# Moving weight preparation earlier and halving the plain part of the Strassen block

## The chip, the cores and the metric

The kernel runs on one core of a Trainium2 chip. The metric is the device time of one execution in microseconds (us), the median of several runs. All engines named here belong to this core: TensorE (PE, with PEld for its weight loads), VectorE (DVE), ScalarE (ACT), GpSimd (POOL) and SyncE (SP). POOL and SP issue nearly all DMA transfers.

## The reference

Three layers follow each other: a retention layer, and two feed-forward layers over its 3072 tokens of 512 features.

```
for t in range(S):                       # retention, 4 x 8 heads, S = 768, D = 64
    state = gamma * state + outer(k[t], v[t])
    y[t] = scale * (q[t] @ state)
x = y as 3072 tokens x 512
h = x @ w_in;  g = h * sigmoid(1.702 h);  x = g @ w_out      # 512 -> 2048 -> 512
h = x @ w_in2; g = max(h, 0) ** 2;        out = g @ w_out2   # 512 -> 2048 -> 512
```

## The kernel before

**Number format.** Every large matrix product is three matmuls in fp32r: each operand is split into a high part, which ACT casts, and a low part, which DVE subtracts; the kernel adds low x high, high x high and high x low in PSUM. All these matmuls are 128x128 by 128x512.

**Stages.** Tokens are worked in blocks. Blocks 0 and 1 of the first feed-forward layer (512 tokens each) go through `up` and `down`, 16 steps f each, with the products written plainly. From token 1024 on the blocks are 1024 tokens wide and use a Strassen-Winograd scheme with seven products in place of eight: `up2` (eight slice pairs p, seven products of six matmuls each for a pair) and `down2` (28 steps u, 12 matmuls each). These blocks are called (0,1), (0,2) for the first layer and (1,0), (1,1), (1,2) for the second.

**The mixed block (0,1)**, tokens 1024 to 2047, is special. The first `PL` of its eight slice pairs are computed plainly in `up_plain` (four steps of 12 matmuls for a pair), while `mixed_x` makes the Strassen operands of x (B12, B22, T1 to T4: sums on DVE, high parts on ACT at L703, low parts on DVE at L704). The remaining pairs go through `up2`. The high and low parts reuse memory of the up weights, so T2 and T4 can only be placed once plain steps have read those weights.

**The making.** The Strassen sums of the weights are made during the kernel by one generator, `make`, which `background(us)` pushes on: each call first puts the ACT instructions that have been queued with `later` into ACT's program, then adds its argument to a credit and runs the generator's steps until the credit is used up; every step's `yield` names what it takes from the credit. `make_first` prepares the first layer in 16 rounds (steps 0.7, 0.7, 0.85, 0.85, and 1.25 for the low part at L286 and its DMA at L287). `make_second` prepares the second layer from 32 raw chunks. A chunk takes 0.45, 0.7 and 0.7 (L138, L143, L151), then 0.6 and 0.6 (L380 to L384), and 1.1 for the low part (L348) and DMA (L349) of the chunk before. When chunk n is begun, `scale(n + 1)` queues the two ACT instructions (L133, L134) on the next raw chunk; the next call of `background` places them. POOL loads the raw chunks (L275, 512 KB each) and writes the results (L287 1024 KB, L349 896 KB). Chunks 0 and 1 are loaded when `make_first` begins, chunk 2 when `make_second` begins, into memory that `make_first`'s pool has used.

In block 1 `background(BG / 2)` is called twice in each step f below 15. In `up_plain` it is called once after each step, in `up2` twice a slice pair (`BGM` in the mixed block, `BGUP` elsewhere), and in `down2` of the first layer at each step u from 12 on (`BGD`).

**Order.** Every engine executes its instructions in the order in which the program places them; a waiting instruction holds up all that stand behind it. After the last call in block 1 the program places the last step of block 1 (`up` with f = 15: GELU at L655, cast at L656, low part at L660), then the casts and low parts of B11 and B21 (L703, L704), then the first plain step, `down` with f = 15 and `finish`.

**PSUM.** `up`, `up_plain` and `down` use two pools (four banks "h", four banks "y"). After `up_plain` they are closed and one pool "ps" of eight banks opens; `bank` hands its banks out in the order of the queue `banks`.

**Down steps.** In `down2`, `sums(u)` (DVE) runs for u < 12 and the x operands of the next block (`x_operands` through `tick`) from u = 12 on; `prepare` casts the operand of step u + 2 (L980 on ACT, L981 on DVE). From u = 20 the product adds into banks that ACT has just copied out (L1012).

Of the kernel before, what the change touches and what calls it, by code (L numbers as in the profile page):

```python
# [10 lines left out]
F32 = mybir.dt.float32  # L11
# [5 lines left out]
ALU = mybir.AluOpType  # L17
PSUM = bass.MemoryType.PSUM

P = 128  # L20
# [7 lines left out]
TB = 512  # L28
# [12 lines left out]
NSTD = 2  # L41
SLOTS = 8
EARLY = 2
BG = 4.7
BGK = 2.55
BGT = 1.45
CV0 = 7
RAWU = 2
FILL = 6
RAWS = 5  # L50
PL = 4
BGUP = (2.15, 2.4)
BGM = 2.8
BGD = 0.62

# [2 lines left out]
B11, B21, B22, T1, T2, T3, T4, B12 = range(8)  # L60
# [4 lines left out]
def tile_retention_then_two_ffns(  # L65
# [346 lines left out]
    def background(us):  # L412

        credit[0] += us
        while acts:
            acts.popleft()()
        while credit[0] > 0:
            c = next(maker, None)
            if c is None:
                credit[0] = min(credit[0], 3.0)  # L420
                return
            credit[0] -= c
# [21 lines left out]
    with tc.manual_schedule():  # L444
# [254 lines left out]
        def pair(i, src):  # L699
            if i not in xh:  # L700
                xh[i] = wa_p.tile([P, 2, TB], F32R, tag="w0", name=f"xh{i}")
                xl[i] = wb_p.tile([P, 2, TB], F32R, tag="w0", name=f"xl{i}")
            nc.scalar.copy(out=xh[i], in_=src)  # L703
            return lambda: v.tensor_tensor(out=xl[i], in0=src, in1=xh[i], op=ALU.subtract)  # L704
# [83 lines left out]

        g = {}
        ps_p = []  # L790
        banks = deque(range(8))

        def gt(q, p):
            key = q, p // 2
# [4 lines left out]
        def mixed_x():  # L799

            (b11, b21), (b12, b22) = xs.pop(NSTD), xs.pop(NSTD + 1)
            yield
            yield
            yield
            low = pair(B12, b12)
            yield
            low()
            low = pair(B22, b22)
            yield
            low()  # L810
            for _ in range(5):
                yield
            v.tensor_tensor(out=b11, in0=b12, in1=b11, op=ALU.subtract)
            low = pair(T1, b11)
            yield
            low()
            yield
            v.tensor_tensor(out=b11, in0=b22, in1=b11, op=ALU.subtract)
            low = pair(T2, b11)
            yield  # L820
            low()
            yield
            v.tensor_tensor(out=b12, in0=b22, in1=b12, op=ALU.subtract)
            low = pair(T3, b12)
            yield
            low()
            v.tensor_tensor(out=b21, in0=b21, in1=b11, op=ALU.subtract)
            yield
            pair(T4, b21)()

        def up_plain():

            x = mixed_x()
            for c in range(2):
                pairs = ((B11, B21), (B12, B22))[c]
                for s in range(2 * PL):
                    f = NQ * (s % 2) + s // 2
                    hi, lo = weights(f, 0)
                    hp = hp_p.tile([P, TB], F32, tag="h", name=f"h{NSTD + c}_{f}")
                    for k in range(KD):  # L840
                        h, e = (t[pairs[k // 2]][:, k % 2] for t in (xh, xl))
                        nc.tensor.matmul(hp, lo[:, k], h, start=(k == 0), stop=False)
                        nc.tensor.matmul(hp, hi[:, k], h, start=False, stop=False)
                        nc.tensor.matmul(hp, hi[:, k], e, start=False, stop=(k == KD - 1))
                    if c == 0 and s == 0:
                        down(NSTD - 1, NF - 1)
                        finish(NSTD - 1)
                        g_ctx.close()
                        wr_p.extend(
                            ctx.enter_context(  # L850
                                tc.tile_pool(name=f"wr{i}", bufs=1, side="left", reuse_waits="tile")
                            )
                            for i in range(EARLY, SLOTS)
                        )
                    if c == 1 and s == 0:
                        fetch()
                    r, p = divmod(f, NQ)
                    nc.scalar.activation(out=gt(QS[2 * r + c], p), in_=hp, func=ACTF.Gelu_apprx_sigmoid)  # L858
                    if c == 1 and s % 4 == 1 and s > 4:
                        thirds(s // 4 - 1)  # L860
                    next(x, None)
                    background(BGK if c == 0 and s not in (4, 5) or c == 1 and s < 2 else BGT)
            for _ in x:
                pass
            first_ctx.close()
            ps_p.append(ctx.enter_context(tc.tile_pool(name="ps", bufs=1, space=PSUM, reuse_waits="tile")))

        def thirds(m):

            t = g[12, m]  # L870
            v.tensor_tensor(out=t, in0=g[22, m], in1=t, op=ALU.subtract)
# [125 lines left out]
        def down2(l, n, loads, tick):  # L997
            xb, yb, zb = {}, {}, {}
            y = {}
            last = (l, n) == blocks[-1]  # L1000

            def store(q, e):
                r, c = q // 10 - 1, q % 10 - 1
                j = 2 * n + c
                row = 2 * r + e
                dst = ykept[j][:, row] if l == 0 else out[row * P:(row + 1) * P, j * TB:(j + 1) * TB]
                (nc.gpsimd if not last else (nc.sync, nc.scalar)[e]).dma_start(out=dst, in_=y[q][:, e])

            def copy(q, e, a):
                if e == 0:  # L1010
                    y[q] = xy_p.tile([P, 2, TB], F32, tag="xy", name=f"o{l}_{n}_{q}")
                nc.scalar.copy(out=y[q][:, e], in_=a[e][0])  # L1012

            def add(q, e, a):
                v.tensor_tensor(out=y[q][:, e], in0=a[e][0], in1=y[q][:, e], op=ALU.add)
                store(q, e)

            def after(i, e, a):
                if i == 1:
                    yb[e] = bank(f"D{l}_{n}_2_{e}")  # L1020
                    nc.scalar.copy(out=yb[e][0], in_=a[e][0])
                elif i == 2:
                    copy(11, e, a)
                    store(11, e)
                elif i == 6:
                    copy(12, e, a)
                elif i == 7:
                    copy(22, e, a)
                    add(22, e, zb)
                elif i == 4:  # L1030
                    copy(21, e, a)
                    store(21, e)
                elif i == 3:
                    add(12, e, a)

            def free(a):
                for e in range(2):
                    banks.append(a[e][1])

            for i in ORDER:  # L1040
                acc = xb if i in (1, 6, 7, 4) else yb if i == 2 else zb
                if i in (1, 5):
                    for e in range(2):
                        acc[e] = bank(f"D{l}_{n}_{i}_{e}")
                for m in range(NQ // 2):
                    gi, gm, hi, lo = ready.popleft()
                    assert (gi, gm) == (i, m)
                    u = 4 * ORDER.index(i) + m
                    if u % 2 == 1 and u < 8:
                        loads(u // 2)  # L1050
                    if u < 12:
                        sums(u)
                    else:
                        tick()
                    prepare(l, n)
                    if l == 0 and u >= 12:
                        background(BGD)
                    for e in range(2):
                        a = acc[e][0]
                        for p in (2 * m, 2 * m + 1):  # L1060
                            w = fetched[l, n, 1, i, p].rearrange("p j (h c) -> p j h c", h=2)
                            wh, wl = w[:, e, 0], w[:, e, 1]
                            s0, s1 = p == 0 and i in (1, 5), p == NQ - 1
                            matmul(a, wl, hi[:, p % 2], s0, False)
                            matmul(a, wh, hi[:, p % 2], False, False)
                            matmul(a, wh, lo[:, p % 2], False, s1)
                        if m == NQ // 2 - 1:
                            after(i, e, acc)
                    for p in (2 * m, 2 * m + 1):
                        del fetched[l, n, 1, i, p]  # L1070
                    fetch()
                    yield
                if i == 2:
                    free(yb)
                elif i == 3:
                    free(zb)
                elif i == 4:
                    free(xb)
# [112 lines left out]
```

## Time and profile before

| what | value |
|---|---|
| median of 3 runs | 1038.77 us (1038.4 to 1039.32) |
| the profiled execution's own time | 1040.23 us |
| its span, first to last instruction | 1037.9 us |
| mean granted TensorE clock | 0.998 |
| busy: PE, PEld, DVE, ACT, POOL | 99%, 81%, 74%, 55%, 11% |
| 16 DMA engines | 281 MB, 271 GB/s over the span |

The span is what the trace shows; the own time of the same execution is 2.3 us longer, and the median of the runs is 1.46 us below that own time. Busy shares are means over the whole span. PE is nearly always busy, so the idle stretches of PE are few and can be looked at one by one.

### The profile page before, as it was taken

The page shows a single profiled execution, that of the slowest core. Times are in us where ns is not written, and L with a number is a line of the kernel's source. Part 1 is how long each engine was busy: PE and PEld are TensorE (multiplying, and loading weights), DVE is VectorE, ACT ScalarE, POOL GpSimd, SP SyncE. Part 2 cuts the span into 40 slices and gives each one's busy share as a digit, 9 for nine tenths or more (in the row PEclk, how much of TensorE's full clock was granted, in tenths as well). Part 3 has the DMA queues.
Part 4 walks back from the last instruction along what each step waited for, and adds up shares of the span by engine and source line. Part 5 has one row for each costly group of instructions (what it writes and reads, how often), then busy time and mean ns, then how long its engine had stood idle before and what let it go on. Part 6 is the DMA issues. An engine that isn't in the chain of part 4 may idle for free.

```text
span 1037.9 us, 15626 instructions
## 1 busy us (share of the span) xinstructions
PE 1024.2 (99%) x5575; PEld 844.7 (81%) x5575; DVE 769.7 (74%) x1065; ACT 575.1 (55%) x928; POOL 111.4 (11%) x167
## 2 busy tenths in 40 slices
PE   8999999999999999999999999999999999999998
PEld 6888888888878887888887888888888888888886
DVE  5888998798898879567879566787445986355953
ACT  4677775444757566466576588564233464233543
POOL 2121210111321001111001211000000001000000
PEclk9999999999999999999999999999999999999999
DMA  9995798866889888999878999877776877767664
GB/s 349 407 397 175 270 314 298 306 239 239 298 263 354 298 264 268 345 363 343 279 264 272 342 374 294 268 229 232 218 192 194 252 236 232 216 196 195 207 200 162
DMA packets 118812, 281.37 MB, mean 271 GB/s; under 512 B 12624, under 2 KB 12752, under 8 KB 118480
## 3 DMA queue, kind: packets, MB, share of 16 engines
q1 hardware_dynamic: 93488, 187.05, 55.2%
q0 software_dynamic: 24672, 92.28, 25.1%
q8 instruction: 44, 0.72, 0.3%
q10 hardware_dynamic: 576, 1.05, 0.3%
q14 instruction: 32, 0.26, 0.1%
HBM read 206.93 MB, written 73.40 MB: 270 GB/s over the span
## 4 chain that ended last, share of the span: by engine, by line
PE 77%; DVE 4%; ACT 1%; issue 1%; DMA 1%; ACTq 0%; DVEq 0%
PE D L878 34%; PE X L878 19%; PE Z L878 9%; PE Y L878 5%; PE y L681 2%; PE y L679 2%; PE y L680 2%; PE h L648 2%; PE h L650 1%; PE h L649 1%; DVE xl L704 1%; DMA kw<-wq 1%; DVE wq L348 1%; DVE gx L981 1%; DVE w L143 0%
## 5 line engine op out<-in xcount | busy, mean ns | idle before, releaser
L878 PE MATMUL D<-gx,r 128*128 128x512 f32 x1680 | 384.7, 390 | 2.6 <-ACT o L1012 2.4
L878 PEld LDWEIGHTS D<-gx,r 128*128 128x128 f32 x1680 | 314.4, 188 | 71.2 <-ACT o L1012 3.2
L981 DVE TENSOR_TENSOR gx<-g,gx 128x1024 fp32r<-128x1024 f32 x140 | 170.5, 1221 | 41.5 <-ACT gx L980 40.8
L980 ACT CAST gx<-g 128x1024 fp32r<-128x1024 f32 x140 | 145.8, 1051 | 90.3 <-PE D L878 85.5
L878 PE MATMUL X<-xh,r 128*128 128x512 f32 x576 | 177.7, 390 | 0.0
L896 ACT COPY g<-X 128x512 f32<-128x512 f32 x108 | 63.3, 586 | 161.6 <-PE X L878 161.5
L901 DVE TENSOR_TENSOR g<-Z,g 128x512 f32<-128x512 f32 x72 | 49.8, 691 | 134.0 <-ACT g L896 100.7
L878 PEld LDWEIGHTS X<-xh,r 128*128 128x128 f32 x576 | 108.4, 188 | 22.6
L878 PE MATMUL X<-xl,r 128*128 128x512 f32 x288 | 112.1, 389 | 0.0
L878 PE MATMUL Z<-xh,r 128*128 128x512 f32 x288 | 88.6, 389 | 0.0
L878 PEld LDWEIGHTS X<-xl,r 128*128 128x128 f32 x288 | 54.2, 188 | 11.3
L878 PEld LDWEIGHTS Z<-xh,r 128*128 128x128 f32 x288 | 54.1, 188 | 11.2
L878 PE MATMUL Z<-xl,r 128*128 128x512 f32 x144 | 56.0, 389 | 0.0
L648 PE MATMUL h<-hl,w 128*128 128x512 f32 x128 | 50.2, 392 | 0.3 <-DVE w L171 0.2
L649 PE MATMUL h<-hl,w 128*128 128x512 f32 x128 | 49.8, 389 | 0.0
L650 PE MATMUL h<-hl,w 128*128 128x512 f32 x128 | 49.8, 389 | 0.0
L681 PE MATMUL y<-gl,w 128*128 128x512 f32 x128 | 49.8, 389 | 0.0
L679 PE MATMUL y<-gh,w 128*128 128x512 f32 x128 | 49.8, 389 | 0.0
L680 PE MATMUL y<-gh,w 128*128 128x512 f32 x128 | 49.8, 389 | 0.0
L878 PE MATMUL Y<-xh,r 128*128 128x512 f32 x144 | 45.3, 396 | 2.2 <-ACT g L858 2.2
L133 ACT ACTIVATE raw<-raw 128x512 f32<-128x512 f32 x64 | 43.2, 675 | 2.4 <-DMA raw<-win 2.4
L349 POOL DMA_DIRECT2D kw<-wq x32 | 30.4, 950 | 129.0 <-DVE w L381 61.4
(112 smaller groups left out, 1545.5 us busy)
## 6 DMA issues: line engine op xcount, KB each, us to landing
r<-kw SPq DMA_DIRECT2D x532, 256.0 KB, 3.4
kw<-wq POOLq DMA_DIRECT2D x32, 896.0 KB, 6.5
unit<-qkv SPq DMA_DIRECT2D x47, 512.0 KB, 9.1
raw<-w POOLq DMA_DIRECT2D x32, 512.0 KB, 6.2
kw<-wh POOLq DMA_DIRECT2D x16, 1024.0 KB, 4.7
kw<-w SPq DMA_DIRECT2D x16, 512.0 KB, 5.1
raw<-win POOLq DMA_DIRECT2D x16, 512.0 KB, 6.6
raw<-wout POOLq DMA_DIRECT2D x16, 512.0 KB, 6.1
```

The costliest lines, as they stand in the source:

```text
L133: nc.scalar.mul(hm, raw[:, :, 1].bitcast(F32), 2.0 ** -112)
L648: nc.tensor.matmul(hp, lo[:, k], xh, start=(k == 0), stop=False)
L649: nc.tensor.matmul(hp, hi[:, k], xh, start=False, stop=False)
L650: nc.tensor.matmul(hp, hi[:, k], xl, start=False, stop=(k == KD - 1))
L679: nc.tensor.matmul(a, lo[:, e], gh, start=s0, stop=False)
L680: nc.tensor.matmul(a, hi[:, e], gh, start=False, stop=False)
L681: nc.tensor.matmul(a, hi[:, e], gl, start=False, stop=s1)
L878: nc.tensor.matmul(a, w, b, start=start, stop=stop, skip_group_check=True)
L896: nc.scalar.copy(out=t, in_=a)
L901: v.tensor_tensor(out=t, in0=a, in1=t, op=ALU.add)
L980: nc.scalar.copy(out=hi, in_=src)
L981: v.tensor_tensor(out=lo, in0=src, in1=hi, op=ALU.subtract)
```

## The change

`PL` goes from 4 to 2: two slice pairs of the mixed block instead of four are computed plainly, six instead of four go through `up2`. `mixed_x` is written anew for eight steps in place of sixteen: the empty steps go, and T3 comes before T2. The argument of `background` in `up_plain` becomes a list of eight values, one for each step. `BG` for block 1 rises from 4.7 to 5.0. In `down2` of the first layer the calls at u = 12 to 22 get nothing, those below 12 get 0.25 and those from 23 on get 2.2. The pool "ps" gets all its eight banks placed when it opens, in order, and the queue begins with banks 4 to 7. The `thirds` calls inside `up_plain` go; `up2` has its own.

```
-BG = 4.7
-BGK = 2.55
-BGT = 1.45
+BG = 5.0
+BGT = (2.4, 1.3, 0.2, 0.2, 0.2, 2.4, 0.2, 2.0)
-PL = 4
-BGUP = (2.15, 2.4)
-BGM = 2.8
-BGD = 0.62
+PL = 2
+BGUP = (2.2, 2.5)
+BGM = 2.75
+BGD = 2.2
+BGE = 0.25
...
-        banks = deque(range(8))
+        banks = deque((4, 5, 6, 7, 0, 1, 2, 3))
...
             (b11, b21), (b12, b22) = xs.pop(NSTD), xs.pop(NSTD + 1)
-            yield
-            yield
-            yield
             low = pair(B12, b12)
             yield
             low()
             low = pair(B22, b22)
             yield
             low()
-            for _ in range(5):
-                yield
             v.tensor_tensor(out=b11, in0=b12, in1=b11, op=ALU.subtract)
             low = pair(T1, b11)
             yield
             low()
-            yield
-            v.tensor_tensor(out=b11, in0=b22, in1=b11, op=ALU.subtract)
-            low = pair(T2, b11)
-            yield
-            low()
-            yield
             v.tensor_tensor(out=b12, in0=b22, in1=b12, op=ALU.subtract)
             low = pair(T3, b12)
+            yield
+            low()
+            v.tensor_tensor(out=b11, in0=b22, in1=b11, op=ALU.subtract)
+            yield
+            low = pair(T2, b11)
             yield
             low()
...
-                    if c == 1 and s % 4 == 1 and s > 4:
-                        thirds(s // 4 - 1)
                     next(x, None)
-                    background(BGK if c == 0 and s not in (4, 5) or c == 1 and s < 2 else BGT)
+                    background(BGT[2 * PL * c + s])
...
             ps_p.append(ctx.enter_context(tc.tile_pool(name="ps", bufs=1, space=PSUM, reuse_waits="tile")))
+            for k in range(8):
+                ps_p[0].tile([P, TB], F32, tag=f"b{k}", name=f"bank{k}")
...
-                    if l == 0 and u >= 12:
-                        background(BGD)
+                    if l == 0:
+                        background(BGD if u >= 23 else BGE if u < 12 else 0)
```

## Rows read from the trace of the kernel before

**Rows 1.** The page, part 1: busy us, share of the span, instructions.
```profile
PE 1024.2 (99%) x5575; PEld 844.7 (81%) x5575; DVE 769.7 (74%) x1065; ACT 575.1 (55%) x928; POOL 111.4 (11%) x167
```

**Rows 2.** Waits of PE: line, releaser, us in total, times, longest.
```profile
PE Y L878 <- ACT g L858: 2.2, 1, 2.2
```

**Rows 3.** Timeline of PE after the plain steps: start, length, work, idle before.
```profile
302.69 0.39 PE L878 MATMUL X<-xl,r 128*128 128x512 f32 x1
305.27 1.11 PE L878 MATMUL Y<-xh,r 128*128 128x512 f32 x2 [2.20 <-ACT g L858]
...
309.02 0.63 PE L878 MATMUL X<-xh,r 128*128 128x512 f32 x2
```

**Rows 4.** Windows: length, busy by engine, granted clock, DMA share, GB/s.
```profile
305.20:307.00 1.80, 1.73 (x4) 1.38 (x5) 1.80 (x5) 1.55 (x3) 0.21 (x1) 0.56 0.84 264
```

**Rows 5.** Chain that ended last: start, us, work; down steps of three blocks.
```profile
346.61 38.26 PE D L878 x168
...
422.53 1.36 PE X L878 x6
...
501.41 40.95 PE D L878 x180
...
576.61 1.36 PE X L878 x6
...
655.49 73.91 PE D L878 x324
```

**Rows 6.** Chain that ended last, 336 to 432 us: what stands before D.
```profile
390.40 0.77 DVE w L151
...
396.58 1.24 DVE xb L724
...
399.84 0.49 ACT o L1012
```

**Rows 7.** Timeline of DVE at the end of block 1 and after it.
```profile
249.10 1.23 DVE L286 TENSOR_TENSOR wh<-wt,wh 128x1024 fp32r<-128x1024 f32 x1 [0.51 <-ACT wh L324]
...
254.22 2.36 DVE L704 TENSOR_TENSOR xl<-x,xh 128x1024 fp32r<-128x1024 f32 x2 [0.26 <-ACT xh L703]
...
262.62 0.43 DVE L138 TENSOR_SCALAR w<-raw 128x512 uint32<-128x512 uint32 x1 [1.65 <-ACT raw L133]
...
268.06 0.76 DVE L151 SCALAR_TENSOR_TENSOR w<-w,raw 128x512 uint16<-128x512 uint16 x1
```

**Rows 8.** Timeline of POOL over the same stretch.
```profile
250.74 0.75 POOL L287 DMA_DIRECT2D kw<-wh  x1 [2.39 <-DVE w L138]
256.26 0.55 POOL L275 DMA_DIRECT2D raw<-win  x1 [4.77 <-issue]
```

**Rows 9.** Line L287, window 250 to 252 us: its one transfer.
```profile
DMA to landing us min/median/max: 4.9/4.9/4.9
```

**Rows 10.** Line L275, window 255 to 262 us: its one transfer.
```profile
DMA to landing us min/median/max: 5.0/5.0/5.0
```

**Rows 11.** Line L275 over the whole span.
```profile
DMA to landing us min/median/max: 3.9/6.5/9.7
```

**Rows 12.** Timeline of ACT at the end of block 1 and after it.
```profile
253.15 2.00 ACT L703 CAST xh<-x 128x1024 fp32r<-128x1024 f32 x2
...
261.92 0.66 ACT L133 ACTIVATE raw<-raw 128x512 f32<-128x512 f32 x1
...
269.97 0.68 ACT L133 ACTIVATE raw<-raw 128x512 f32<-128x512 f32 x1 [2.15 <-DMA raw<-win]
...
271.10 0.58 ACT L858 ACTIVATE g<-h 128x512 f32<-128x512 f32 x1
```

**Rows 13.** The plain steps' first matmul line, L842.
```profile
L842 PE MATMUL h<-xh,w x64: 389/389/389, 255.3 to 300.9; 128*128 128x512 f32 x64
```

**Rows 14.** Windows of slice pairs 5 and 6 in the mixed block.
```profile
320.50:330.00 9.50, 9.50 (x44) 7.87 (x43) 8.06 (x18) 5.89 (x11) 3.04 (x4) 1.00 1.00 343
330.00:339.50 9.50, 9.50 (x44) 7.87 (x43) 8.04 (x12) 7.67 (x13) 0.96 (x1) 1.00 1.03 396
```

More of the change, by code (lines that the diff above doesn't have):

```diff
@@ L816, in mixed_x @@
             low()
-            yield
-            v.tensor_tensor(out=b11, in0=b22, in1=b11, op=ALU.subtract)
-            low = pair(T2, b11)
+            v.tensor_tensor(out=b12, in0=b22, in1=b12, op=ALU.subtract)
+            low = pair(T3, b12)
             yield
             low()
+            v.tensor_tensor(out=b11, in0=b22, in1=b11, op=ALU.subtract)
             yield
-            v.tensor_tensor(out=b12, in0=b22, in1=b12, op=ALU.subtract)
-            low = pair(T3, b12)
+            low = pair(T2, b11)
             yield
```

## The prediction

> **What bounds the kernel now.** The page's first part shows PE busy for 99% of the span [rows 1], so the time is PE's work plus its few gaps. I then read PE's waits, its timeline at the largest one, the chain of waits through the down steps, and the timelines of DVE, POOL and ACT where block 1 passes into the plain steps. The reader is to see three things. Of all that PE waits for after the retention layer, the largest single wait is that of the first Y product of the mixed block for a GELU of the last plain step [rows 2]. The down steps of the two first-layer blocks are longer than those of a second-layer block, though they hold the same matmuls [rows 5]. And at the end of block 1 the engines are close to the edge: DVE has the low part of B11 ready only just before PE needs it [rows 7, 13].
>
> **Fewer matmuls.** A group of six matmuls takes 1.36 us [rows 5], 0.227 us each. A plain slice pair has four steps of 12, 48 matmuls; a Strassen pair has seven products of six, 42. Two pairs change sides: 2 x 6 x 0.227 = **2.7 us less**.
>
> **The wait of Y.** From 302.69 to 309.25 us PE issued 11 intervals of matmuls [rows 3] (the last row holds two, 0.63 - 0.39 apart), which at 0.227 take 2.5 us: the wait with its slow restart costs 4.1 us. In the restart the granted clock is 0.56 of full, the lower of the two levels, 1.2 GHz [rows 4]. GELU was late because ACT first had to do the cast of T3, which waited for DVE, and three making instructions. With the change X, Y and Z of the first pair take banks of the old "y" pool, copied out many us before, and ahead of the last GELU there is no cast that waits: the last one, T2, stands two steps before, and T4's comes after the GELU. Should a bank still tie Y to that GELU, it runs 0.6 us after the plain matmuls, inside the 1.36 us of X. **4.1 us less**, at worst 3.8.
>
> **The down steps.** 27 steps of 12 matmuls take 75.92 us in the mixed block (346.61 to 422.53), 75.20 in (0,2) (501.41 to 576.61) and 73.90 in (1,0), where nothing is made [rows 5]. The 2.0 and 1.3 us above that come mostly at u = 20: the making steps (L151 among them) push the sum for T2 (L724) back on DVE, ACT waits for it, and the bank copies behind it end 0.04 us before PE goes on at 400.37 [rows 6]. With no call from u = 12 to 22 the block is there as (1,0) is. The small 0.25 calls fall where a step's DVE work is a sum and a low part, 2 x 1.2 (half of 2.36, [rows 7]) of 2.72 us. From u = 23 on the x operands are done, and three low parts (1.2 each) and 5 x 2.2 of making, 14.6 us, stand against 13.6 of PE; operands are prepared two steps (5.4 us) ahead. So **3.3 us less**; bounds 0 (the same work shifted) and 3.6.
>
> **Block 1 and the first plain step.** This is what the sum hangs on. Credit: the making gets 31 calls by the end of block 1, 31 x 2.35 = 72.9 before and 31 x 2.5 = 77.5 now. `make_first` takes 16 x 4.35 = 69.6. Before, 3.3 is left: chunk 0's own steps (3.05). Now 7.9 is left: chunk 0, all of chunk 1 (4.15), and the first two steps of chunk 2. Chunk 1 is begun in the first call of f = 14; so in the second call of f = 14 the scaling of raw chunk 2 (L133, L134) enters ACT's order. Behind it stand GELU and cast of f = 15 and the casts of B11 and B21. Before, even chunk 1's scaling came after these: it runs at 261.92, the casts at 253.15 [rows 12].
>
> Raw chunk 2 cannot be there. Its load uses memory of `make_first` and waits for the landing of that stage's last write. Before: write issued at 250.74, landing 4.9 us later at 255.6 [rows 8, 9]; load issued at 256.26 after an idle of 4.77, landing 5.0 later, 261.3 [rows 8, 10]. Now the last low part of that stage runs with one low part of `up` fewer ahead of it (f = 14's stands behind), 0.6 us earlier: 248.5 in place of 249.10 [rows 7], and the only idle time of DVE there, 0.51 us for ACT's cast [rows 7], stays. So write 250.1, landed 255.0, load 255.7, landed 260.7. That ACT does wait for such a landing, with all behind it, is shown at 269.97, 2.15 us [rows 12].
>
> From 260.7 ACT needs 1.13 for L133 and L134 (269.97 to 271.10), some 0.5 for GELU and 0.6 for its cast (estimates from these rows' neighbours) and 1.0 for B11 [rows 12]: 264.0. PE would have begun the first plain step at 255.3 [rows 13]. Its third matmul, planned at 255.8, also needs DVE's low part of B11, 1.2 us more (half of 2.36, [rows 7]): 265.3. That is 9.5 us. The slow restart of rows 3 lasts 3.7 us with a matmul each 0.43; part of it passes while PE waits for the low part, so I add 6 matmuls x 0.2 = 1.2. **10.7 us more.** Bounds: with the fastest landing of the line (3.9) 9.6, with the slowest (9.7) 15.4 [rows 11]; its median would make it 12.2. I take 5.0, that of this very load at the same place.
>
> The Trainium skill, page "DMA: Bandwidth & Descriptors", section "Anatomy of one DMA — SWDGE (gpsimd) path", gives a transfer about 2.0 us plus its bytes over 436 GB/s: by it, as an estimate, 4.4 us for the 1024 KB write and 3.2 for the 512 KB load. The first is near the 4.9 of rows 9, the second well below the 5.0 of rows 10. By the page the price would be 2.3 us smaller and the sum 2.3 lower; the measured landings decide.
>
> **The rest of the mixed block.** After that stall the plain steps take 2.72 us each and everything else has caught up; the operands follow in the order of the new `mixed_x`. The chain of DVE and ACT (T3, T2, T4, each sum 1.2, cast 1.0, low part 1.2) ends close before the first pair. Its making call then places a cast (L386) that waits for DVE behind T4's low part, and the copy for the first X7 stands behind it: by adding these lengths up it is some 1.0 us late. Six pairs with 5.5 of making, in place of four with 5.6, keep the DMA engines full longer [rows 14]; 0.3 for that. **1.3 us more**, bounds 0 and 4. The other edits (BGUP up by 0.05 and 0.1 a call) fall into slack: DVE's total in a slice pair, near 8 of 9.5 us [rows 14], grows by 0.2; without that slack they would cost that much.
>
> **Sum.** -2.7 - 4.1 - 3.3 + 10.7 + 1.3 = +1.9. The profiled execution's span goes from 1037.9 to 1039.8 and its own time from 1040.2 to 1042.1; the median of the runs stands 1.5 below that: **1040.7 us**.
>
> **The rivals.** (a) *The load is there in time.* Then ACT waits for nothing, but DVE's order still holds chunk 1 and two steps of chunk 2 (262.62 to 268.06, 5.4 us, [rows 7]) and a low part of 0.6 ahead of B11's. It would start at 248.5 + 4.9 + 6.0 = 259.4 and end at 260.6, 4.9 after PE's need, with restart 6.1: -10.1 + 6.1 + 1.3, 1036.1 us. For it speaks that landings vary; against it that two landings in a row would have to take 4 us in all where they took 10. (b) *The late start costs nothing:* the plain steps begin as before, -10.1 + 1.3, 1030 us, faster. Against it stands DVE's queue; it takes an ordering other than I read. (c) *The down steps keep their excess:* the five calls of 2.2 hold ACT and DVE at the passage to the next block, or the operands alone are late at u = 20; 3.3 us come back, 1044.0, slower. Against it speaks the block without making. It decides as soon as 0.2 us of the 3.3 are lost, given the rest. (d) *Weight reads arrive late.* A slice pair then asks for seven reads of 256 KB and 1.33 chunks of 1.41 MB, 3.7 MB in 9.5 us, 390 GB/s; the two rows moved 343 and 396 at a share of 1.0 [rows 14]. At 343 the lag grows by 1.3 us a pair; eight buffers cover 9.5 us from issue to use, so the fifth and sixth pair would wait, some 2.5 us: 1043.2, slower.
>
> **How the numbers follow.** A measurement of this kernel tells a change from none at about 0.2%, 2.1 us: below 1036.7 is faster, above 1040.9 slower. My forecast gets 0.60; its own range is 1037.5 to 1043.5 by the bounds of the landing and of the down steps, and it divides into 0.04 faster, 0.35 same, 0.21 slower. (a) gets 0.13 (0.10 faster, 0.03 same), (b) 0.06 faster, (c) 0.12 and (d) 0.09 slower. Together: faster 0.20, same 0.38, slower 0.42. The range 1034.0 to 1044.5 leaves out (b) and the upper tails of (c), (d) and of the landing, below 0.2.
>
> **What would show it.** Right: an idle stretch of PE of 8 to 9 us before the second or third matmul of the first plain step, ACT's L133 just before GELU of f = 15, waiting for DMA, and the granted clock near 0.56 after it; no wait of Y for L858; down steps of about 74 us in (0,1) and (0,2). Wrong: the plain steps begin near 255 us, or L133 stands behind the casts of B11; then the time falls below 1037. If the down steps stay at 75 to 76 us, or X and Z wait for reads of weights, it lies above 1042.

## The result: slower by 0.9%, outside the forecast range

The changed kernel takes 1048.38 us in the median of its runs (1047.29 to 1050.4), the kernel before, beside it, 1039.05 us: ratio 1.0091, 95% interval 1.0079 to 1.0103. The forecast was 1040.7, with 1044.5 as the upper end. The profiled execution took 1047.29 us with a span of 1045.5, against 1040.23 and 1037.9 before. Of the miss of 7.7 us the span holds 5.7 (+7.6 in place of +1.9). The other 2.0 are in neither trace: this execution was 1.1 us below its median where that of before stood 1.46 above, 2.5 together, less 0.5 that lie between span and own time. Executions differ by about that much: of 69 runs of the kernel before beside the experiments, 40 with a mean granted clock of 0.999 or 1.0 have a median span of 1036.6 us, 29 with a lower clock 1038.4, and the profiled execution (0.998) is like these.

The page of the changed kernel, part 1, beside [rows 1]: PE executes 12 matmuls fewer and is busy as long as before.

```profile
PE 1025.1 (98%) x5563; PEld 841.4 (80%) x5563; DVE 772.4 (74%) x1071; ACT 578.2 (55%) x934; POOL 111.0 (11%) x167
```

The waits of PE in the changed kernel from 250 to 660 us (line, releaser, us in total, times, longest), beside [rows 2]. The wait of Y for the GELU of L858 is gone. In its place stand one long wait in front of the plain steps and six for reads of weights (`r<-kw`, the line of `fetch`), of a kind that before did not have.

```profile
PE h L836 <- ACT xh L703: 6.8, 1, 6.8
PE X L872 <- ACT g L890: 1.2, 2, 0.9
PE X L872 <- DMA r<-kw: 1.1, 3, 0.5
PE y L681 <- DVE gl L660: 0.9, 1, 0.9
PE Z L872 <- DMA r<-kw: 0.7, 2, 0.4
PE Y L872 <- DMA r<-kw: 0.4, 1, 0.4
```

**The start of the plain steps.** Timeline of PE in the changed kernel (start, length, work, idle before), then of ACT and of POOL over the same stretch, to be read beside [rows 7, 8 and 12].

```profile
256.97 0.40 PE L681 MATMUL y<-gl,w 128*128 128x512 f32 x1
264.21 0.79 PE L836 MATMUL h<-xh,w 128*128 128x512 f32 x1 [6.84 <-ACT xh L703]
264.81 0.63 PE L837 MATMUL h<-xh,w 128*128 128x512 f32 x1
265.48 0.79 PE L838 MATMUL h<-xl,w 128*128 128x512 f32 x1
```

```profile
260.88 0.65 ACT L133 ACTIVATE raw<-raw 128x512 f32<-128x512 f32 x1 [5.78 <-DMA raw<-win]
261.44 0.65 ACT L134 ACTIVATE raw<-raw 128x512 uint32<-128x512 uint32 x1
261.99 0.57 ACT L655 ACTIVATE gs<-h 128x512 f32<-128x512 f32 x1
262.60 0.62 ACT L656 CAST gh<-gs 128x512 fp32r<-128x512 f32 x1
263.12 1.99 ACT L703 CAST xh<-x 128x1024 fp32r<-128x1024 f32 x2
```

```profile
251.54 0.75 POOL L287 DMA_DIRECT2D kw<-wh  x1 [2.39 <-DVE w L138]
256.92 1.09 POOL L275 DMA_DIRECT2D raw<-win  x2 [4.62 <-issue]
```

Read from below: the last write of `make_first` (L287) goes out at 251.54; the load that waits for its landing goes out 5.4 us later; ACT stands 5.78 us at L133 for that load, and GELU, its cast and the casts of B11 and B21 stand behind. PE goes on at 264.21 where it began the plain steps at 255.31 before [rows 13], and the first matmuls are slow. Windows of the changed kernel (columns as in [rows 4]):

```profile
264.10:266.00 1.90, 1.75 (x3) 1.00 (x4) 1.81 (x2) 1.01 (x2) 0.00 (x0) 0.50 0.90 304
266.00:270.60 4.60, 4.60 (x18) 3.67 (x17) 1.25 (x2) 0.10 (x1) 0.00 (x0) 0.80 0.28 97
```

**The down steps and the ups.** Chain that ended last in the changed kernel, to be read beside [rows 5].

```profile
352.53 73.60 PE D L872 x324
426.13 1.36 PE X L872 x6
...
431.61 4.41 PE X L872 x18
...
447.54 1.63 PE Z L872 x6
...
502.21 2.72 PE D L872 x12
```

The 27 down steps of (0,1) are 73.60 us now, without a break. But from the first X of (0,2) at 426.13 to its first down step at 502.21 pass 76.08 us, where 54 products of 1.36 us are 73.44. The same stage of (1,0) takes 76.27.

**Where the time went, by stage.** Each stage runs from its first matmul to the first of the next; the starts are PE's matmul starts in the two traces, and each loss is the difference of two lengths.

| stage | before | after | difference |
|---|---|---|---|
| first plain matmul at | 255.31 | 264.21 | +8.90 |
| plain steps with `down` f = 15 (17 steps of 12, then 9) | 46.24 | 26.49 | beyond 2.72 a step: 0, then 2.01: +2.01 |
| ups of (0,1) (26 products, then 40) | 39.46 | 56.23 | beyond 1.36 each: 4.07, then 1.78: -2.29 |
| matmuls saved in these two stages | | | -2.70 |
| downs of (0,1) | 81.36 | 79.04 | -2.32 |
| ups of (0,2) | 73.44 | 76.08 | **+2.64** |
| downs of (0,2) | 80.63 | 79.07 | -1.56 |
| ups of (1,0) | 73.44 | 76.27 | **+2.83** |
| from the first down step of (1,0) to the last matmul | 383.90 | 383.88 | -0.02 |
| sum | | | +7.49 |

### The profile page after: what moved, and what is told of

The parts are those of the page before. It is cut to its first block, busy times and chain, and to the rows that moved or that the text cites. A ratio compares the mean times of both kernels' runs of the same rounds, so it can differ in the third digit from the quotient of the medians.

```text
span 1045.5 us, 15658 instructions
## 1 busy us (share of the span) xinstructions
PE 1025.1 (98%) x5563; PEld 841.4 (80%) x5563; DVE 772.4 (74%) x1071; ACT 578.2 (55%) x934; POOL 111.0 (11%) x167
## 4 chain that ended last, share of the span: by engine, by line
PE 68%; DMA 3%; ACT 1%; issue 1%; DVE 1%; POOL 0%; POOLq 0%; DVEq 0%; ACTq 0%
PE D L872 35%; PE X L872 18%; PE Z L872 9%; PE Y L872 4%; DMA r<-kw 2%; DMA raw<-wout 1%; ACT xh L703 0%; DMA raw<-win 0%; DVE xl L704 0%; ACT raw L134 0%; DVE wq L348 0%; ACT raw L133 0%; ACT wq L386 0%; PE h L836 0%; PE h L838 0%
## 5 line engine op out<-in xcount | busy, mean ns | idle before, releaser
L872 PE MATMUL X<-xh,r 128*128 128x512 f32 x608 | 188.5, 391 | 2.5 <-ACT g L890 1.2
L895 DVE TENSOR_TENSOR g<-Z,g 128x512 f32<-128x512 f32 x76 | 52.5, 691 | 138.6 <-ACT g L890 101.8
L890 ACT COPY g<-X 128x512 f32<-128x512 f32 x114 | 66.6, 585 | 156.7 <-PE X L872 156.7
L872 PEld LDWEIGHTS X<-xh,r 128*128 128x128 f32 x608 | 113.3, 188 | 29.9 <-ACT g L890 3.5
L872 PE MATMUL X<-xl,r 128*128 128x512 f32 x304 | 118.4, 389 | 0.0
L872 PE MATMUL Z<-xh,r 128*128 128x512 f32 x304 | 93.8, 390 | 0.7 <-DMA r<-kw 0.7
L872 PEld LDWEIGHTS Z<-xh,r 128*128 128x128 f32 x304 | 56.9, 188 | 13.3 <-issue 0.8
L872 PEld LDWEIGHTS X<-xl,r 128*128 128x128 f32 x304 | 57.1, 188 | 11.8
L872 PE MATMUL Z<-xl,r 128*128 128x512 f32 x152 | 59.2, 389 | 0.0
L133 ACT ACTIVATE raw<-raw 128x512 f32<-128x512 f32 x64 | 43.2, 675 | 7.8 <-DMA raw<-win 6.7
```

The costliest lines, as they stand in the source:

```text
L133: nc.scalar.mul(hm, raw[:, :, 1].bitcast(F32), 2.0 ** -112)
L872: nc.tensor.matmul(a, w, b, start=start, stop=stop, skip_group_check=True)
L890: nc.scalar.copy(out=t, in_=a)
L895: v.tensor_tensor(out=t, in0=a, in1=t, op=ALU.add)
```

## Experiments

The times are medians beside runs of the kernel before on the same chip (1038.95 to 1039.61). Stage lengths are read from each kernel's trace as above.

### late2: the two calls of f = 14 behind the casts

```
-                if f < NF - 1:                        # in up
+                if f < NF - 1 and (n, f) != (1, NF - 2):
-                if f < NF - 1 and cv["b"] == len(order):
+                if f < NF - 1 and cv["b"] == len(order) and (n, f) != (1, NF - 2):
         for low in lows:
             low()
+        background(BG / 2)
+        background(BG / 2)
```

> The changed kernel, with the two making calls of f = 14 of block 1 taken from their places and put behind the low parts of B11 and B21; nothing else differs, and the credit given is the same. Theory (the late start of the plain products is ScalarE standing at the scaling of raw chunk 2, with the casts of B11 and B21 behind it): the casts issue as soon as the last gelu part of block 1 is out, TensorE's first plain matmul comes within 2 us of the 255.3 us of the kernel before in place of 264.2, no wait of TensorE on a cast is over 1 us, and the time falls by 8 to 11 us, to 1037 to 1040. Rival (VectorE's backlog or the load itself holds the operands, and moving the calls only moves who is named): first plain matmul still after 262 us, time 1045 to 1048. A third outcome: the start is early but the making, now later, is late for the weight reads of the mixed block, and 3 us or more come back there.

Measured 1040.17 us, ratio to before 1.0007 (0.9998 to 1.0015), 8.2 us below the changed kernel. Timeline of ACT in late2:

```profile
255.94 2.00 ACT L703 CAST xh<-x 128x1024 fp32r<-128x1024 f32 x2
257.84 0.68 ACT L133 ACTIVATE raw<-raw 128x512 f32<-128x512 f32 x1
258.41 0.68 ACT L134 ACTIVATE raw<-raw 128x512 uint32<-128x512 uint32 x1
258.97 0.94 ACT L386 CAST wq<-w 128x896 fp32r<-128x896 f32 x1
261.17 0.69 ACT L133 ACTIVATE raw<-raw 128x512 f32<-128x512 f32 x1 [1.26 <-DMA raw<-win]
```

The casts now stand ahead of both scalings, and the wait for the load at 261.17 holds up nothing that PE needs. The first plain matmul comes at 257.15. The theory holds; the gain is at the lower end because GELU's low parts still end late (below), and because 1.1 of the 8.2 us that the trace wins ahead of the ups of (0,1) are lost again in the ups of (0,2) and (1,0), 76.76 and 76.72 us.

### late1: only the second call moved

The same edit for the second call alone, the one that places the scaling of raw chunk 2.

> The changed kernel with only the second making call of f = 14 put behind the low parts of B11 and B21; the first one stays. Theory (the second call places the scaling of raw chunk 2 ahead of the casts, and that wait is what starts the plain steps late): ScalarE no longer waits for the load ahead of the casts, the first plain matmul comes between 255 and 258 us; what VectorE still has of chunk 1 ahead of B11's low part holds the third matmul to 259 or 260, so the wait is 2 to 5 us in place of 9. Rival (VectorE's steps of chunk 1, which wait for raw chunk 1's scaling, hold it as much as ScalarE did): third plain matmul still after 263.

One run: 1040.07 us. First plain matmul at 257.01, the third at 259.19 after a wait of 1.4 us for VectorE's low part of B11. So the 9 us are ScalarE's queue; VectorE's steps of chunk 1 are worth some 1 us beside it (26.34 us for the plain stage, 25.36 in late2).

### even and early: the same 11 us of making elsewhere in the downs

```
-                        background(BGD if u >= 23 else BGE if u < 12 else 0)
+                        background(11 / 16 if u >= 12 else BGE)                 # even
+                        background(BGD if 12 <= u < 17 else BGE if u < 12 else 0)  # early
```

> The changed kernel, with the 11 us of making credit of a down stage's last five steps (2.2 each, steps 23 to 27) given as 0.69 at each of its last sixteen steps (12 to 27), as the kernel before places it; sum and everything else are as in the changed kernel. Theory (11 us of making packed right ahead of the ups fills the DMA engines with loads and stores just when the ups' reads begin, so that reads land later than eight buffers cover): TensorE's waits for reads in the ups of (0,2) and (1,0) go, each of these stages shrinks from 76.1 and 76.3 to about 73.5 us, -5.3; the down stages get their excess of about 1.6 and 2.3 back; in sum -1 to -2.5 us against the changed kernel, 1046 to 1047.5. Rival (it is the total of making, or the larger credit within the ups, 2.2 and 2.5 for 2.15 and 2.4): both ups stay at 76 us and the down excess returns, +3.9, 1052.

> The changed kernel, with the same five credits of 2.2 us given at steps 12 to 16 of the down stage in place of 23 to 27; all else is the same. Theory (distance to the ups matters): as packed as before but 11 steps (some 30 us) ahead of the ups, so the reads of the ups of (0,2) and (1,0) are back in time, 73.5 each, -5.3; the five steps now stand beside the x operands of the next pair on VectorE and ScalarE, which costs the down stages 1 to 4 us; in sum -4 to -1, 1044.5 to 1047.5. Rival (packing as such, wherever it is): the reads of the down stage itself are late at steps 12 to 20 by about as much as those of the ups were, and the sum is within 1 us of the changed kernel.

| | time | downs (0,1) | ups (0,2) | downs (0,2) | ups (1,0) |
|---|---|---|---|---|---|
| after | 1048.38 | 79.04 | 76.08 | 79.07 | 76.27 |
| even | 1048.18 | 82.49 | 73.44 | 81.82 | 73.44 |
| early | 1060.05 | 88.17 | 73.44 | 87.60 | 73.44 |

In both the late reads are gone from the ups, as the theory says. Its sums were wrong: even pays 6.2 us in the downs, not 3.9, and early 17.7, not 1 to 4. Waits of PE in early, 250 to 660 us:

```profile
PE D L872 <- DVE gx L975: 11.8, 10, 2.0
PE h L836 <- ACT xh L703: 6.9, 1, 6.9
PE D L872 <- ACT o L1006: 2.1, 2, 1.1
```

At steps 12 to 16 VectorE makes the x operands; the making ahead of them makes the low parts of the down operands (`gx`) late ten times. This place is the worst of all, and the rival for early (late reads at the same steps) is wrong too: the wait is for DVE.

### noload: the making without part of its bytes

```
             m, i = jobs[n]
             k = n % len(raw_p)
+            if n >= 12:
+                raws[n] = raws[n - 3]
+                return
```

> The changed kernel without the loads of raw chunks 12 to 31: each of these chunks works on what is in its buffer, so the second layer's weights, and with them the output, are not the reference's. All instructions of the making on VectorE and ScalarE and its stores stay where they are; only 512 KB of the 1.41 MB that a chunk moves goes. Theory (the reads are late because the making's transfers fill the DMA engines): the waits for reads in the ups of (0,2) and (1,0), 2.6 and 2.8 us, fall below 0.5 us each, the stages to 73.4 to 74 us, and reads land within 9 us of their issue. Rival (the making's instructions hold up the engines, buffers come free late and reads are issued late): the stages stay at 75.5 us or more.

One run: 1042.18 us; the ups of (0,2) and (1,0) take 73.44 us each, and PE waits for no read. Reads of L766 (L769 in noload) in the first 30 us of the ups of (0,2), issue to landing; first the kernel before, then the changed one, noload, and late2up (below):

```profile
DMA to landing us min/median/max: 3.2/5.2/7.1
```
```profile
DMA to landing us min/median/max: 4.6/8.7/11.4
```
```profile
DMA to landing us min/median/max: 2.8/4.8/7.5
```
```profile
DMA to landing us min/median/max: 3.7/5.9/7.1
```

The making's instructions on VectorE and ScalarE and its stores are all there; without 512 KB a chunk the reads are in time. So it is the making's bytes, not its instructions. By the starts of the matmuls, 0.9 of the 5.5 us in the changed kernel stand at waits for ScalarE's copies of X (at 431.61 and 586.99) and 4.4 at reads; noload has neither. With eight buffers a read is used some 9.5 us after its issue (seven products of 1.36); of the reads issued from 10 us before the ups of (0,2) to 30 us into them, seven take longer than that in the changed kernel, and none in the kernel before, noload and late2up. Windows of the changed kernel, then of noload, in the same part of the stage (the last three columns: clock, DMA share, GB/s):

```profile
430.00:440.00 10.00, 9.96 (x44) 7.90 (x44) 6.64 (x17) 6.35 (x11) 2.38 (x4) 1.00 1.04 415
440.00:450.00 10.00, 8.78 (x36) 6.07 (x35) 3.90 (x8) 5.88 (x10) 1.11 (x2) 1.00 1.04 409
```
```profile
430.40:440.40 10.00, 10.00 (x45) 8.27 (x45) 6.98 (x17) 5.82 (x11) 1.76 (x2) 1.00 1.02 391
440.40:450.40 10.00, 10.00 (x46) 8.26 (x45) 5.93 (x12) 6.30 (x12) 1.06 (x2) 1.00 0.90 306
```

### late2up, late2low, late2u20: a smaller burst

All three start from late2.

```
-BGUP = (2.2, 2.5)
-BGD = 2.2
+BGUP = (2.5, 2.8)                      # late2up
+BGD = 1.0
-BGD = 2.2
-BGE = 0.25
+BGD = 1.36                             # late2low
+BGE = 0.6
-     background(BGD if u >= 23 else BGE if u < 12 else 0)
+     background(11 / 8 if u >= 20 else BGE if u < 12 else 0)   # late2u20
```

> The kernel late2 with the making moved from the last five down steps into the ups: BGD 1.0 in place of 2.2, BGUP 2.5 and 2.8 in place of 2.2 and 2.5; the sum of the credit is about the same. Theory (it is the packing of 11 us of making right ahead of the ups that makes the reads late, not the amount): with 5 us there the waits for reads in the ups of (0,2) and (1,0) fall from 3.3 us each to under 1, the down stages stay at 73.5 us, and the time is 5 to 6.5 us below late2, 1034 to 1035. Rival (the DMA engines are full in these ups in any case, share 1.0, and what is asked for there counts): the waits stay or grow, 1040 or more.

> The kernel late2 with part of the making of the last five down steps moved to the first twelve: BGD 1.36 in place of 2.2, BGE 0.6 in place of 0.25; the sum is the same. Theory: the burst ahead of the ups shrinks from 11 to 6.8 us and the reads' waits from 3.3 us to about 1 in each of the two ups, -4.5; VectorE, which shows no idle time in steps 4 to 11, falls behind with the operands there, +0 to +4; sum -4.5 to 0 against late2, 1035.5 to 1040. Rival (amount over the whole stage counts, not its place): waits for reads unchanged and a wait for gx added, 1040 to 1044.

> The kernel late2 with the 11 us of making of the last five down steps spread over the last eight: 1.375 from step 20 on. Theory (the loads and stores come some 4 us earlier on average and drain before the ups' reads): waits for reads in the two ups fall to 1 to 2 us each, -3 to -4.5; the wait at step 20 for the bank copies behind the sum of T2, which the kernel before shows, comes back with 1 to 2 us a stage, +2 to +4; sum -2 to +1 against late2. Rival (packing over eight steps is as bad as over five): waits for reads as in late2 and +2 to +4.

| | time | ratio to before | downs (0,1) | ups (0,2) | downs (0,2) | ups (1,0) |
|---|---|---|---|---|---|---|
| late2 | 1040.17 | 1.0007 | 78.99 | 76.76 | 79.07 | 76.72 |
| late2up | 1034.28 | 0.9948 (0.9934 to 0.9962) | 79.06 | 73.44 | 79.00 | 73.62 |
| late2low | 1036.62 | 0.9968 (0.9956 to 0.9981) | 79.97 | 75.14 | 79.74 | 73.44 |
| late2u20 | 1037.45 | 0.9978 (0.9968 to 0.9987) | 79.14 | 74.55 | 79.05 | 74.91 |

late2up is faster than both kernels: it asks for more making in the ups, 2.5 and 2.8 a call, and less right ahead of them, and PE waits for no read. The amount in the ups is not what counts; the rival falls. In late2u20 the wait at step 20 did not come back, so the downs have room for 1.4 us a step from there; 1.1 and 1.5 us of late reads stay in the ups, as its theory had it. In late2low reads are late in (0,2) and not in (1,0), with the same 6.8 us of credit ahead of both. All waits of PE that late2up has left from 250 to 660 us:

```profile
PE X L874 <- ACT g L892: 0.9, 1, 0.9
PE y L681 <- DVE gl L660: 0.9, 1, 0.9
PE h L840 <- DVE xl L704: 0.5, 1, 0.5
```

### banks and nobanks: the part on PSUM

banks is the kernel before with this part of the change alone, nobanks the changed kernel without it.

```
-        banks = deque(range(8))
+        banks = deque((4, 5, 6, 7, 0, 1, 2, 3))
...
+            for k in range(8):
+                ps_p[0].tile([P, TB], F32, tag=f"b{k}", name=f"bank{k}")
```

> The kernel before with one part of the change alone: the eight PSUM banks are taken in the order 4 to 7, 0 to 3, and each is placed once at the start of the mixed ups. Theory: the 2.2 us wait of the first Y product for a gelu goes, and with it the slow restart, together 4.1 us: 1034 to 1036 us. Rival (the wait is for ScalarE's backlog, which the bank order only moves to another product): the first Y no longer waits but the next product that reads fresh data does, time 1038 to 1039.5, the same as before.

> The changed kernel with the bank part of the change undone: banks in the order 0 to 7, none placed at the start. Theory (what took the 4.1 us out of the mixed ups is that ScalarE is no longer late with the last plain GELU, whatever bank the first Y takes): from the first X to the first D the stage takes 56.2 us as in the changed kernel, within 0.5, and no wait of Y is over 0.5 us. Rival (the bank order is needed beside it): a wait of the first Y of 0.6 to 2.5 us with a slow restart, the stage 57 to 60 us.

banks: 1039.82 us, ratio 1.0007 (0.9998 to 1.0017). nobanks: one run, 1049.08; its ups of (0,1) take 56.23 us, as with the banks. So this part is worth nothing here, alone or with the rest; in banks the rival is right. The waits of PE in banks, beside [rows 2]:

```profile
PE X L880 <- ACT g L898: 2.9, 1, 2.9
PE D L880 <- ACT o L1014: 2.4, 2, 1.3
```

Y waits no more, but product 6 adds into X's bank, which ScalarE must have copied out, and that copy stands behind the same late GELU. ScalarE was late, not the bank.

### downs and beforeup: the placing of the making alone, in the kernel before

```
-                    if l == 0 and u >= 12:
-                        background(BGD)
+                    if l == 0:
+                        background(2.2 if u >= 23 else 0.25 if u < 12 else 0)   # downs
+                        background(1.0 if u >= 23 else 0.25 if u < 12 else 0)   # beforeup
-BGUP = (2.15, 2.4)
+BGUP = (2.5, 2.8)                                                               # beforeup
```

> The kernel before with the down part of the change alone: no making credit at steps 12 to 22 of a down stage, 0.25 below 12, 2.2 from 23 on. Theory (the down stages gain what the forecast said and the ups behind them lose more): down stages of (0,1) and (0,2) from 78.7 and 77.9 us to about 76.3, together -3.5 to -3.9; ups of (0,2) and (1,0) from 73.4 to 76 us each by waits for reads, +5 to +6.5; sum +1 to +3, 1040.5 to 1042.5. Rival (the late reads of the changed kernel need its later raw chunks or larger credits in the ups as well): only the down gain, -3.5, 1036.

> The kernel before with the making placed as in late2up and nothing else of the change: credit of the down stages 0.25 below step 12, none to 22, 1.0 from 23 on; in the ups 2.5 and 2.8 in place of 2.15 and 2.4. Theory (late2up gains from two sources that add: 3.9 us from the down stages and some 2 us from two plain pairs fewer): the down part alone, -3.5 to -4 us, 1035 to 1036, so late2up stays ahead by 1 to 2 us. Rival (all of late2up's gain is the placement of the making): 1034 to 1034.5. Rival (the down gain needs the changed kernel's earlier making): no change.

downs: 1043.54 us, ratio 1.0030 (1.0019 to 1.0041): downs -1.8 and -1.6, ups +1.2 and +6.2. beforeup: 1036.17 us, ratio 0.9964 (0.9952 to 0.9976). The part of the change that was to save time in the downs makes the kernel slower by itself, and the same part with a smaller burst makes it faster. late2up stays 1.9 us ahead of beforeup in the medians, with intervals of the ratios that overlap. That this is what two plain pairs fewer are worth is not shown: the two spans are 2.8 us apart (1034.88 and 1032.07), and by stages late2up gains 2.7 by fewer matmuls, 1.0 in the ups of (0,1), 1.4 in those of (1,0), and loses 2.2 up to the end of the plain stage (it starts 1.4 later and takes 0.8 more beyond its matmuls). The ups of (1,0) take 74.96 us in beforeup: ScalarE's copies of X are late there, and of the reads around the start of the stage none takes longer than 7.2 us.

### late2up47 and late2mix: a smaller BG

From late2up: `BG = 4.7` for 5.0, with `BGUP = (2.7, 3.1)` (late2up47) or `BGE = 0.5` (late2mix).

> The kernel late2up with BG 4.7 in place of 5.0 in block 1 and the credit given back in the ups, BGUP 2.7 and 3.1 in place of 2.5 and 2.8. Theory (the larger BG makes VectorE late with two low parts of GELU, a gap of some 1 us at 254.9 and one of 0.7 in the first plain step): both gaps go, -1 to -1.7; the ups still have no wait for reads over 0.5 us; 1032.5 to 1033.5. Rival (the ups are at their edge): waits for reads return with 1 us or more a stage, 1034 to 1037.

> The kernel late2up with BG 4.7 in place of 5.0 in block 1 and the credit given back in the first twelve down steps, BGE 0.5 in place of 0.25. Theory (the larger BG makes VectorE late with GELU's last low parts): the gap of 1.0 us at 254.9 and that of 0.7 in the first plain step go, the ups keep 73.4 us, 1032.5 to 1033.5. Rival (with less credit by the end of block 1 the mixed block's ScalarE order is worse, as in late2up47, whose third product waited 2 us for a copy): the gain is given back there, 1034 to 1035.

1037.35 us (0.9974, 0.9964 to 0.9984) and 1037.25 us (0.9979, 0.9970 to 0.9988). The gaps at the end of block 1 do go: the first plain matmul comes at 256.07 and 255.04, 257.29 in late2up, and the plain stage takes 24.48 us for 25.29. But the ups of (0,1) grow by 1.8 and 1.3, and the making not done in block 1 is paid for later. Waits of PE in late2up47, then in late2mix:

```profile
PE X L874 <- ACT g L892: 6.2, 5, 1.9
```
```profile
PE X L874 <- ACT g L892: 2.8, 3, 1.4
PE X L874 <- DMA r<-kw: 1.3, 2, 0.9
PE D L874 <- DMA r<-kw: 1.0, 2, 0.5
```

In late2up47 the copies of X on ScalarE are late in the ups of (1,0), which take 78.08 us, and not in those of (0,2), 73.44, with the same 3.1 a call. At 2.8 the stage of (1,0) takes 73.62 in late2up, 74.20 in late2mix and 74.96 in beforeup, so the ups of (1,0) are near the end of what they bear. The theory's gain was real and smaller than what was given back.

late2mix also shows what the credit does not tell. It gives the last five down steps 1.0 a call, as late2up does, and yet reads are late in the ups of (0,2): 76.05 us, with reads of up to 11.6 us. These ups begin at 416.89. From 407.96 to 418.63 POOL issues two stores (407.96, 414.69) and two loads (410.00, 418.63) of the making; late2up, whose ups begin at 417.86, issues one of each there (414.35, 413.35). What is issued ahead of the reads counts; the credit of the last steps tells it only roughly.

## Why the prediction was wrong

**Right, and in size: block 1 and the first plain step.** Forecast 10.7 (9.5 and a restart of 1.2), measured 8.9 and 2.0, 10.9 together. late2 and late1 show the cause that was named, raw chunk 2's scaling ahead of the casts. The parts moved against each other: write and load were later than worked out (251.54 and 256.92 for 250.1 and 255.7) and the load landed in 3.9 us, not 5.0; the restart lasted longer. Of that load the Trainium skill, page "DMA: Bandwidth & Descriptors", section "Anatomy of one DMA — SWDGE (gpsimd) path", gives 3.2 us as an estimate from its figures; this trace shows 3.9, [rows 10] 5.0. Putting that scaling behind the casts gives back 8.2 of the 10.9 (late2). The other 2.7 have a cause that no term held, hidden behind the first: with the larger BG VectorE is late with GELU's low parts and B11's, and with BG 4.7 the plain stage begins at 255.04 and takes 24.48 us (late2mix).

**Right: matmuls saved**, -2.7.

**Right in sum, with a reason that was half wrong: the wait of Y.** -4.1 and +1.3 were forecast for the ups of (0,1), -2.3 in all was measured. Of the two reasons that the prediction gave, banks and nobanks leave only the second: no cast that waits stands ahead of the last GELU. The late copy ahead of the first X7 came as worked out: PE waits 0.9 us for it at 297.32, forecast 1.0.

**Right in size, and bought elsewhere: the down steps.** Forecast -3.3, measured -3.9; with no call from step 12 to 22 they run as where nothing is made. Here is **the step that failed**: "From u = 23 on ... 14.6 us, stand against 13.6 of PE". It weighed the five calls of 2.2 on VectorE and ScalarE alone, where they do fit, and put what they issue at nothing. By the prediction's own steps a chunk is 4.15 us of credit and 1.41 MB, so 11 us are 2.65 chunks, 3.7 MB of loads and stores put right ahead of the ups' own reads; the trace shows three stores and three loads of the making between 420.25 and 430.45, around the start of the ups at 425.97. That costs 2.6 us in (0,2) and 2.8 in (1,0), 5.5 that no term held (4.4 at reads, 0.9 at copies of X behind the same burst). even, noload and late2up show it from three sides: spread the calls, take away a third of the bytes, or halve the burst, and both stages are back at 73.4 to 73.6. late2low and late2mix show that the credit is a rough measure of the bytes.

**Rival (d) had the mechanism and the wrong place.** It put late reads into the fifth and sixth pair of the mixed block, by the traffic of a steady slice pair, with 2.5 us and a chance of 0.09. In the mixed block no read was late. The lag did not grow with the steady rate; it came from the burst at the border of two stages, twice.

**BGUP "falls into slack"** is right: even keeps 2.2 and 2.5, and both stages take 73.44 us as before. At 2.5 and 2.8 the ups of (0,2) stay at 73.44 in late2up and beforeup, and those of (1,0) lose 0.2 and 1.5.

**The other rivals.** The load was not in time (a), the late start was not free (b), the downs did not keep their excess (c).

**A second step failed: "the median of the runs stands 1.5 below that".** It carried this distance of the kernel before over to the changed one, whose median stands 1.1 above its profiled execution. That makes 2.0 of the miss of 7.7. The distance is near the length of the slow restart after the wait of Y (1.9 of the 4.1 us), and the change takes that wait away. beforeup keeps the wait, 2.13 us, without a slow restart, and its ups of (0,1) take 38.13 us for 39.46; so it is likely that not every execution of the kernel before has this restart. No other execution of it has a trace here, and it is not shown.

**Left open.** Why the clock falls after the wait of Y in one trace and not in another. In downs the ups of (1,0) lose 6.2 us and those of (0,2) 1.2: by the starts of the matmuls about 2.4 of the 6.2 stand at waits for ScalarE and VectorE and 3.4 at reads; why that stage is hit harder was not looked into.

## What to carry to other kernels

Background work has a price on every resource that it uses: count the bytes that it issues, and put them beside the reads of the stage that follows, not only beside the instructions of the stage in which it is placed. Background work that must be done by a deadline is cheapest where it is spread over the stage with engine time to spare and packed nowhere; here 0.3 us more a call in the ups cost 0.2 (late2up), and 11 us in five steps ahead of them cost 5.5. Before a buffer or a bank is blamed for a wait, look which engine is late: moving the buffer may only move the wait to the next product.

## What the runs showed of the hardware that was not expected

- The DMA share does not tell whether reads are late. In windows of 10 us at a share of 1.02 to 1.04 the reads landed in at most 7.1 us at 368 to 396 GB/s (late2up, first window below) and in up to 11.4 us at 409 to 415 GB/s (the changed kernel, above). The rate of a window does not draw the line sharply either: in late2mix the slowest read took 11.6 us, in windows at 286 GB/s (407 to 417 us, share 0.91) and 402 GB/s (417 to 427, share 1.03).

```profile
417.90:427.90 10.00, 10.00 (x46) 8.29 (x45) 6.10 (x12) 5.59 (x10) 2.42 (x4) 1.00 1.03 386
427.90:437.90 10.00, 10.00 (x46) 8.29 (x45) 6.42 (x13) 6.41 (x12) 1.51 (x2) 1.00 1.04 368
437.90:447.90 10.00, 10.00 (x46) 8.29 (x45) 7.06 (x13) 7.15 (x13) 1.49 (x2) 1.00 1.02 396
```

- After PE had stood for 6.84 us the granted clock was 0.50 for the first 1.9 us, the lower level of 1.2 GHz, and 0.80 in the mean of the next 4.6. After the 2.2 us of [rows 3] it was 0.56. But the length of a wait alone does not tell: in beforeup Y waits 2.13 us for the same GELU, and the clock stays 1.00 (window below, beside [rows 4]). And after the same stop of 6.8 to 6.9 us the plain stage took between 26.36 us (early) and 27.89 (nobanks), so the restart is not of one length. In late2 PE waits 0.9 and 0.5 us at this place, and the whole plain stage, 25.36 us, is only 0.9 above 9 x 2.72.

```profile
305.70:307.50 1.80, 1.68 (x7) 1.08 (x7) 1.80 (x5) 1.57 (x3) 0.18 (x1) 1.00 0.90 303
```
